# Scores gathered into one stretch per batch, with most of feed-forward-1 cut into 64-row quads, in an attention and feed-forward kernel on one core

## The chip, the cores and the metric

The kernel runs on one core of a Trainium2 chip. The metric is device time in microseconds (us) of one execution, lower is better. Most runs of one kernel agree within about 0.3%. The time includes about 2 us outside the span of the profile: 427 us of time goes with a span of 425 us. All runs of the changed and the edited kernels are of the fast state (mean granted TensorE clock 0.99 to 1.0), and runs of one table line were timed on the same chip as the kernel before.

Names of engines in the profile: PE is TensorE's matmuls, PEld its weight loads, DVE VectorE, ACT ScalarE, POOL GpSimd, SP SyncE (here only a queue for DMA).

## The reference, cut to what matters

```python
# q: (8 batches, 16 heads, 384, 64); k, v: (8, 4, 384, 64); w_in: (1024, 2048); w_out: (2048, 1024)
k, v = np.repeat(k, 4, axis=1), np.repeat(v, 4, axis=1)
scores = np.matmul(q, k.transpose(0, 1, 3, 2)) / np.sqrt(64)
attn = softmax(scores)
x = np.matmul(attn, v)                        # "AV"; then rows of all heads side by side: (3072, 1024)
h = np.maximum(x @ w_in, 0.0)                 # "feed-forward-1"
out = (h * h) @ w_out                         # "feed-forward-2"
```

The contraction of scores has 64 elements, that of everything else 128 or a multiple of it. So scores fill only half of the rows of the 128 x 128 array. The kernel lays one head's keys on rows 0 to 63 and another's on rows 64 to 127 and lets two matmuls of 64 rows run side by side, as two tiles of the array.

## The kernel before

A recorder collects every operation with what it reads and writes, orders TensorE's work by a model of time, and inserts semaphores. Per batch TensorE does 12 units of scores, 8 of AV (18 matmuls each), 16 tiles of feed-forward-1 (8 matmuls of 384 columns each) and 6 groups of feed-forward-2 (16 matmuls of 512 columns each). From batch 1 on, scores came in bursts of two units. A burst fills six of the eight banks of PSUM, and one wide exp empties them:

```python
    def burst_two(b, u):
        def sc(pe):
            for k0, cols in ((0, ((0, 512), (512, 768))), (1, ((0, 256), (256, 768)))):
                for c0, c1 in cols:
                    for x in range(2):            # x = 0: rows 0..63 of the array, x = 1: rows 64..127
                        flat = ps[:, 3 * x:3 * x + 3, :].rearrange("p n c -> p (n c)")
                        m = pe.matmul(flat[:, k0 * HC + c0:k0 * HC + c1],
                                      kT[b % 2][64 * x:64 * x + 64, u + k0, :],
                                      q_cols(b, (u + k0) // NJ, x, c0, c1))
            return m
        # ... PE writes banks 0..5; one ACT exp of 3072 elements a partition reads them all
```

Feed-forward-1 used the whole array, in banks 6 and 7, and split its work after the matmul between two engines:

```python
            def mm(pe):                            # one half of a tile: k0..k1 of 8 chunks
                for kc in range(k0, k1):
                    m = pe.matmul(bank(i)[:, 0:S], w_in_sb[:, kc, c * 128:(c + 1) * 128],
                                  xT[b % NXT][:, kc, :], start=(kc == 0), stop=(kc == NKC - 1))
                return m
                # ... after the last chunk:
                R.add("vector", lambda e: e.tensor_scalar_max(hr[r][:, :], bank(i)[:, 0:S], 0.0), ...)
                R.add("scalar", lambda e: e.activation(h2T[b % 2][:, c, :], hr[r][:, :], AF.Square), ...)
```

A list scheduler picks the next piece for TensorE; scores of batch b+1, AV of batch b+1 and feed-forward of batch b are mixed as they become ready:

```python
        if sc_q:
            # ... b > 0:
                ok = ok and not held & set(LOW)
                t = max(R.when(reads=score_reads(b, u) + score_reads(b, u + 1)) + 3.0 * (b == 2),
                        R.when(writes=[("bank", i) for i in LOW]))
        # ...
        ready = [x for x in cand if x[0] <= now + 0.05]
        what = min(ready, key=lambda x: x[1]) if ready else min(cand)
```

The softmax here doesn't subtract the row's maximum and nothing guards it: scores larger than these inputs give would overflow.

## Time and profile before

| | |
|---|---|
| time, median of 4 runs | 427.08 us (426.95 to 427.46) |
| span of the profiled run | 425.1 us |
| TensorE busy | 99% of the span |
| VectorE, ScalarE busy | 37%, 46% |
| score bursts in batches 1 to 7 | 42 |

Lines of the profile's page follow. Some records of matmuls are missing (755 of line 496 below, where the program has 784); a step that spans a missing record was read as two. First comes the table of busy times: busy us, share of the span, instructions of each engine. Then the chain of work that ended last, then groups of instructions: line, engine, operation, output<-inputs, shapes, count | busy us, mean ns of one | idle time of the engine before them.

```profile
PE 419.2 (99%) x3435; PEld 231.1 (54%) x3464; DVE 157.7 (37%) x332; ACT 194.8 (46%) x194; POOL 55.3 (13%) x68
...
PE 96%; DMA 1%; issue 1%; ACT 1%; POOL 1%; DVE 0%; POOLq 0%
...
L440 PE MATMUL ps<-xT,w_in_sb 128*128 128x384 bf16 x1024 | 174.8, 326 | 0.0
L496 PE MATMUL ps<-w_out_sb,h2T 128*128 128x512 bf16 (+2 forms) x755 | 167.5, 375 | 1.9 <-issue 0.5
L368 ACT ACTIVATE expT<-ps 128x3072 bf16<-128x3072 f32 x42 | 114.5, 2727 | 64.4 <-PE ps L358 63.7
...
L383 PE MATMUL ps<-v_aug,expT 128*128 128x65 bf16 x1152 | 41.2, 193 | 0.0
...
L358 PE MATMUL ps<-qT,kT 64*128 64x512 bf16 (+1 forms) x336 | 34.6, 325 | 0.0
```

TensorE has next to no idle time, and 96% of the chain is TensorE: only less work on TensorE, or denser work, can help. The "mean ns" of a matmul is no cost, as matmuls overlap. The cost is the step from one start to the next.

The timeline of TensorE in the kernel before. Columns: start us, us until the last of the run ends, engine, line, what, count.

```profile
128.60 0.82 PE L358 MATMUL ps<-qT,kT 64*128 64x512 bf16 x8
129.36 3.42 PE L440 MATMUL ps<-xT,w_in_sb 128*128 128x384 bf16 x20
132.62 1.26 PE L383 MATMUL ps<-v_aug,expT 128*128 128x65 bf16 x36
133.72 1.46 PE L440 MATMUL ps<-xT,w_in_sb 128*128 128x384 bf16 x8
135.11 0.82 PE L358 MATMUL ps<-qT,kT 64*128 64x512 bf16 x8
135.87 3.42 PE L440 MATMUL ps<-xT,w_in_sb 128*128 128x384 bf16 x20
```

Read it by start times. Twenty matmuls of line 440 start at 129.36 and the next kind at 132.62: 163 ns each. The Trainium skill ("TensorE: Matmul & The Clock Gate", Back-to-back issue gap) gives columns / 2.4 GHz + 2.5 ns for a single matmul with a warm clock, here 162.5 ns; the trace agrees. But the eight from 133.72 to 135.11, where a score burst follows, take 1.39 us instead of 1.30. The score burst from 135.11 to 135.87 takes 0.76 us, where its columns need 0.65. From the start times of single matmuls, the step into a burst is 258 ns after a 384-column matmul (163 elsewhere) and 312 after one of 512 columns (216 elsewhere); out of a burst it is 308 instead of 216. I call each such change between whole array and 64-row tiles a border. Over the 84 borders the median loss is 96 ns. The first step behind a border is about 10 ns slow as well (226 ns for a pair of 512 columns).

### The profile page before, as it was taken

Reading aid. Unit: us, or ns where it says so; the run is one execution under the profiler, and the core shown is the slowest. Engines: PE = TensorE matmul, PEld = TensorE weight load, DVE = VectorE, ACT = ScalarE, POOL = GpSimd, SP = SyncE. Lnnn points to the kernel's source line nnn. Section 1 sums busy time; section 2 is a strip of 40 time slices with the busy share of each in tenths; the row PEclk is TensorE's granted clock in tenths of the full one; section 3 lists DMA queues with packets and bytes.
Section 4 is the critical chain, followed back from the end, with each engine's and each line's share of the span. In section 5 each row is a group of like instructions: output and inputs, shape, how many; then the busy total and the mean of one; then the engine's idle time right before and its main releaser. Section 6 shows DMA issues by size and latency. Waiting matters only on the chain.

```text
span 425.1 us, 7813 instructions
## 1 busy us (share of the span) xinstructions
PE 419.2 (99%) x3435; PEld 231.1 (54%) x3464; DVE 157.7 (37%) x332; ACT 194.8 (46%) x194; POOL 55.3 (13%) x68
## 2 busy tenths in 40 slices
PE   8999999999999999999999999999999999999997
PEld 6665554555545555455554455544554465446544
DVE  3564331443324443244442344432441244114312
ACT  6957720477255773557745377552340034003300
POOL 8680001234012004004000000000000000000000
DMA  9999999999689179838918321033001100110012
GB/s 180 190 189 201 186 200 228 173 152 172 136 182 167 26 106 131 144 100 133 116 45 180 104 23 25 18 93 91 25 2 49 74 26 2 49 74 26 1 68 81
DMA packets 96915, 44.30 MB, mean 104 GB/s; under 512 B 77296, under 2 KB 90864, under 8 KB 96880
## 3 DMA queue, kind: packets, MB, share of 16 engines
q0 software_dynamic: 36544, 17.44, 32.2%
q1 hardware_dynamic: 59664, 25.86, 28.7%
q8 instruction: 27, 0.44, 0.4%
q10 hardware_dynamic: 672, 0.49, 0.4%
q14 instruction: 8, 0.07, 0.1%
HBM read 35.65 MB, written 12.58 MB: 113 GB/s over the span
## 4 chain that ended last, share of the span: by engine, by line
PE 96%; DMA 1%; issue 1%; ACT 1%; POOL 1%; DVE 0%; POOLq 0%
PE ps L440 40%; PE ps L496 39%; PE ps L383 8%; PE ps L358 7%; DMA q_st<-in_q_dram 1%; PE ps L337 1%; ACT expT L347 1%; PE ps L311 0%; PE ps L416 0%; PE ps L294 0%; POOL q_st L239 0%; POOL v_st L232 0%; DVE qT L318 0%; DVE y_sb L505 0%; POOL ident L523 0%
## 5 line engine op out<-in xcount | busy, mean ns | idle before, releaser
L440 PE MATMUL ps<-xT,w_in_sb 128*128 128x384 bf16 x1024 | 174.8, 326 | 0.0
L496 PE MATMUL ps<-w_out_sb,h2T 128*128 128x512 bf16 (+2 forms) x755 | 167.5, 375 | 1.9 <-issue 0.5
L368 ACT ACTIVATE expT<-ps 128x3072 bf16<-128x3072 f32 x42 | 114.5, 2727 | 64.4 <-PE ps L358 63.7
L440 PEld LDWEIGHTS ps<-xT,w_in_sb 128*128 128x128 bf16 x1024 | 97.1, 98 | 69.5 <-issue 6.8
L450 ACT ACTIVATE h2T<-hr 128x384 bf16<-128x384 f32 x128 | 64.5, 520 | 140.7 <-DVE hr L448 140.5
L496 PEld LDWEIGHTS ps<-w_out_sb,h2T 128*128 128x128 bf16 x784 | 73.7, 98 | 87.1 <-issue 5.1
L448 DVE TENSOR_SCALAR hr<-ps 128x384 f32<-128x384 f32 x128 | 71.2, 557 | 106.3 <-PE ps L440 106.3
L505 DVE COPY y_sb<-ps 128x512 f32<-128x512 f32 (+2 forms) x49 | 33.3, 681 | 122.6 <-PE ps L496 122.6
L383 PEld LDWEIGHTS ps<-v_aug,expT 128*128 128x128 bf16 x1152 | 39.3, 98 | 6.9 <-issue 0.6
L383 PE MATMUL ps<-v_aug,expT 128*128 128x65 bf16 x1152 | 41.2, 193 | 0.0
L398 DVE TENSOR_TENSOR o_sb<-ps,rinv 128x384 bf16<-128x384 f32 x64 | 35.6, 557 | 2.2
L358 PE MATMUL ps<-qT,kT 64*128 64x512 bf16 (+1 forms) x336 | 34.6, 325 | 0.0
L358 PEld LDWEIGHTS ps<-qT,kT 64*128 64x128 bf16 x336 | 13.0, 94 | 20.7 <-issue 6.3
L392 DVE RECIPROCAL rinv<-ps 128x6 f32<-128x6 f32 x64 | 12.2, 190 | 27.0 <-PE ps L383 27.0
L271 POOL COPY v_aug<-v_st 128x768 bf16<-128x768 bf16 x8 | 6.6, 831 | 84.1 <-PE ps L383 69.3
L347 ACT ACTIVATE expT<-ps 128x1024 bf16<-128x1024 f32 (+1 forms) x20 | 16.9, 981 | 0.7 <-PE ps L337 0.6
L266 POOL COPY k_dup<-k_st 128x1536 bf16<-128x1536 bf16 x7 | 10.3, 1470 | 42.7 <-DMA k_st<-in_k_dram 42.7
L239 POOL DMA_DIRECT2D q_st<-in_q_dram x17 | 14.8, 886 | 0.9 <-POOLq L751 0.8
L207 POOL DMA_DIRECT2D k_st<-in_k_dram x7 | 5.3, 758 | 39.1 <-DMA qT<-q_st 39.1
L337 PE MATMUL ps<-qT,kT 64*128 64x384 bf16 (+2 forms) x48 | 7.2, 330 | 0.6 <-DVE qT L318 0.2
L249 POOL DMA_DIRECT2D w_in_sb<-in_moe_w_in_dram x8 | 7.1, 895 | 0.0
L232 POOL DMA_DIRECT2D v_st<-in_v_dram x8 | 6.3, 790 | 0.1
(26 smaller groups left out, 41.5 us busy)
## 6 DMA issues: line engine op xcount, KB each, us to landing
out_dram<-y_sb SPq DMA_DIRECT2D x47, 256.0 KB, 2.0
q_st<-in_q_dram POOLq DMA_DIRECT2D x14, 384.0 KB, 8.5
w_in_sb<-in_moe_w_in_dram POOLq DMA_DIRECT2D x8, 512.0 KB, 14.3
w_out_sb<-in_moe_w_out_dram POOLq DMA_DIRECT2D x4, 1024.0 KB, 30.2
v_st<-in_v_dram POOLq DMA_DIRECT2D x8, 192.0 KB, 10.4
k_st<-in_k_dram POOLq DMA_DIRECT2D x7, 192.0 KB, 4.4
q_st<-in_q_dram POOLq DMA_DIRECT2D x3, 192.0 KB, 5.0
xT<-o_sb SPq DMA_TRANSPOSE x28, 2.9
```

The lines of the kernel that those rows point to most:

```text
L239: R.add("gpsimd", lambda g: g.dma_start(q_st[st][:, h0:h1, :], q[b, h0:h1].rearrange("h (p j) d -> p h (j d)", j=NJ)), writes=[("q_st", st ...
L347: R.add("scalar", lambda e: e.activation(dst, src, AF.Exp, scale=0.125), reads=keys, writes=[("expT", (b * NU + u) % NEX, t) for u, _, _ i ...
L358: m = pe.matmul(flat[:, k0 * HC + c0:k0 * HC + c1], kT[b % 2][64 * x:64 * x + 64, u + k0, :], q_cols(b, (u + k0) // NJ, x, c0, c1))
L368: R.add("scalar", lambda e: e.activation(dst, src, AF.Exp, scale=0.125), reads=keys, writes=[("expT", (n + m) % NEX, t) for m in range(2) ...
L383: m = pe.matmul(po[:, f - 6 * s2, 0:D + 1], w, v_aug[b % 2][:, g * NJ + j, 0:D + 1], start=(j == 0), stop=(j == NJ - 1))
L392: R.add("vector", lambda e: e.reciprocal(rinv[r].ap().unsqueeze(2), po[:, :, D:D + 1]), reads=[("bank", i)], writes=[("rinv", r)], cost=0.13)
L398: R.add("vector", lambda e: e.tensor_tensor(dst, srcv, rbv, ALU.mult), reads=[("bank", i), ("rinv", r)], writes=[("o_sb", o, s2)], cost=0.48)
L440: m = pe.matmul(bank(i)[:, 0:S], w_in_sb[:, kc, c * 128:(c + 1) * 128], xT[b % NXT][:, kc, :], start=(kc == 0), stop=(kc == NKC - 1))
L448: R.add("vector", lambda e: e.tensor_scalar_max(hr[r][:, :], bank(i)[:, 0:S], 0.0), reads=[("bank", i)], writes=[("hr", r)], cost=0.48)
L450: R.add("scalar", lambda e: e.activation(h2T[b % 2][:, c, :], hr[r][:, :], AF.Square), reads=[("hr", r)], writes=[("h2T", b % 2, c)], cost ...
L496: m = pe.matmul(bank(i)[:, 0:n], h2T[b % 2][:, c, i3 * 128:(i3 + 1) * 128], w_out_sb[:, c, c0:c1], start=(c == 0), stop=(c == NFC - 1))
L505: R.add("vector", lambda e: e.tensor_copy(ysl, bank(i)[:, 0:n]), reads=[("bank", i)], writes=[("y", yb)], cost=0.08 + n / 960)
```

## The change

Its intent is to have TensorE change between whole-array matmuls and 64-row tiles twice per batch instead of twelve times. To have something to run beside the scores in the same mode, feed-forward-1 is cut into 64-row halves. A "quad" works on four tiles in banks 4 to 7. In phases 0 and 1 the two halves of the array work on different tiles, in phases 2 and 3 they swap, so that each tile gets both halves of its contraction. Scores go in small pieces through banks 0 to 3. The run of scores and quads of one batch is called its stretch. AV and feed-forward-2 then run on the whole array. VectorE now makes the squares of the quads. The core of the diff:

```diff
-    NST, NEX, NXT, NHR, NY = 2, 8, 3, 4, 3
+    NST, NEX, NXT, NHR, NY, NO = 2, NU, 2, 4, 3, 6
...
-    def burst_two(b, u):      # (removed; scores use burst_small, two banks and exps of 1024 elements)
...
+    def quad(b, tiles):
+        rs, ends = [], {}
+        def part(phase, k0):
+            xs = ((0, 1), (2, 3), (1, 0), (3, 2))[phase]
+            def piece():
+                def mm(pe):
+                    for kc in range(k0, k0 + 4):
+                        for x in range(2):
+                            c, r = tiles[xs[x]], slice(64 * x, 64 * x + 64)
+                            m = pe.matmul(bank(4 + xs[x])[:, 0:S], w_in_sb[r, kc, c * 128:(c + 1) * 128],
+                                          xT[b % NXT][r, kc, :], start=(phase < 2 and kc == 0),
+                                          stop=(phase > 1 and kc == NKC - 1))
+                    return m
+                ...
+                for i in sorted(xs):          # after phases 2 and 3
+                    R.add("vector", ... e.tensor_scalar_max(hr[r][:, :], bank(4 + i)[:, 0:S], 0.0) ...)
+                for c, r in rs if phase == 3 else ():
+                    R.add("vector", ... e.tensor_tensor(h2T[:, c, :], hr[r][:, :], hr[r][:, :], ALU.mult) ...)
...
+            if b and not split:     # a stretch opens only at an edge, with four tiles or more left
+                ok = ok and at_edge and (u > 0 or pairs >= 8 * b and ff["b"] == b - 1 and len(ff["tiles"]) >= 4)
...
+                t = max(R.when(reads=reads) + 3.0 * (b == 2 and not split), R.when(writes=[...two banks...]))
...
+        if split:
+            inside = [x for x in cand if x[2] in ("sc", "ffn")]
+            if not at_edge or inside and min(inside)[0] <= now + 0.3:
+                cand = inside
```

In the resulting order 100 of the 128 feed-forward-1 tiles run as quads: 12 beside the scores of batch 1, 8 beside those of batch 2, 16 beside those of batches 3 to 7.

## The prediction

> **What bounds it now.** TensorE. The first table of the page gives PE 99% of the 425.1 us span; the chain of waits is 96% PE, with feed-forward-1 40%, feed-forward-2 39%, AV 8%, the score bursts of batches 1 to 7 7%. VectorE is busy 37%, ScalarE 46%. Start-to-start steps of matmuls in the trace: feed-forward-1 163 ns (384 columns), feed-forward-2 216 ns (512), AV 29 ns, a pair of 64-row score matmuls 109 ns per 256 columns. Each is columns/2.4 GHz plus about 2.5 ns, so there is no slack inside a run of one kind.
>
> **What the change removes.** The visible loss is at the border between whole-array matmuls and 64-row tiles. Into a burst the step is 258 ns where 163 is normal, or 312 where 216 is normal: 95 ns. Out of it 308 ns, where a 512 pair takes 216: 92 ns. The first pair inside takes 227 instead of 216. The Trainium skill ("TensorEngine Tiling (Array Packing)", Key Properties) says a change of tiling mode drains the array; this trace agrees, at about 94 ns. Before: 42 bursts, 84 borders, about 8.3 us with the slow first pairs. In the changed order of instructions I count 20 borders in batches 1 to 7 (two per batch, eight in batch 2, whose scores outlast its quads). 64 fewer: 64 x 94 ns = 6.0 us, and 0.4 us of slow first pairs. All of it is on the critical path, as PE never rests.
>
> **What it adds or moves.** 100 of 128 feed-forward-1 tiles run as quads: 1600 half-height matmuls in 800 pairs. The bursts show pairs at the rate of one whole-array matmul and weight loads (94 ns, two at once) hidden, so I expect 162 to 165 ns a pair: 0 to 1.5 us. Exps become 1024 elements wide, 1.06 us (batch 0) against half of 2.73: 18 x 1.06 = 19 us per stretch, under the stretch's 20.8 + 3.9 = 25 us of PE, so ScalarE should not stall PE. Squares move to VectorE: per quad four relus and four multiplies at a step of about 0.48 us (557 ns recorded, overlapping) = 3.9 us against 5.2 to 6.3 us of PE. It fits, but tightly at one place: two banks come free about 1.46 us after the last matmul start of a phase (0.36 release + 0.48 + 0.56 + signal), and the phase after next wants them after 1.46 us. Where no score piece lies between, up to 0.1 us waits: 0 to 2 us. AV begins behind a VectorE backlog of about 3 us; six banks and four feed-forward-2 matmuls cover most of it: about 0.5 us. Start and last batch stay as they were. w_in chunk 3 lands at 30.4 us and is wanted at about 30.6.
>
> **Prediction.** 427.1 - 6.4 + about 1.6 = **422.0 us**; 8 in 10: 419.8 to 425.6. Faster by over 2%: 0.04; within 2%: 0.90; slower by over 2%: 0.06.
>
> **What would show it.** Right: about 20 steps of 258 to 312 ns at borders; a quad pair's step at 162 to 165 ns; PE still 99%; VectorE's share up by about 10 points, ScalarE's down about 7; waits of PE's weight loads for VectorE and ScalarE summing under 3 us. Wrong: a pair step well over 165 ns; PE waits for the relus or the exps of several us; VectorE near full in the stretches.
>
> **What could make it wrong.** The multiply on two fp32 operands costing more than 0.5 us a step; half-height weight loads not hidden beside longer streams (each 10 ns on a pair costs 8 us); q/k transposes arriving late now that a batch wants all scores at once; the two-bank release being later than I read.

## The result, and the profile after

| kernel | time, median (range) | against the kernel before |
|---|---|---|
| before | 427.08 us (426.95 to 427.46) | |
| changed | 423.50 us (423.38 to 425.05) | 0.9923, 95% interval 0.9899 to 0.9947 |

A ratio here and below is the mean time of one kernel's fast runs over that of the other's of the same rounds, so it is not quite the ratio of the medians quoted. The change makes the kernel 0.8% faster: 3.6 us. That lies in the predicted range, and the verdict is "same" at the 2% line.

The profile fell on the slowest of the four runs (425.05 us). Its TensorE waited 1.6 us for the first queries at about 9 us, where its repeat (e5 below, 423.74 us) waited 0.6 us. From 11.05 us on its trace also records half the clock for 3.41 us, and e5's trace does not. In the thirteen traces such a stretch at half clock, before the work ends, follows only pauses of TensorE of 1.6 to 2.0 us (here, in e6, and twice in e3); no pause of 1.45 us or less has one. Four cases don't make a rule. Such differences of the start come and go in all kernels here. So I also compare the profiles from a fixed point on: from the run of feed-forward-1 ahead of batch 1's scores to the end of the last matmul. That is 397.4 us in the kernel before and 393.4 us in the changed one, 4.0 us less. The lines of its page:

```profile
PE 414.9 (98%) x4241; PEld 236.9 (56%) x4264; DVE 198.4 (47%) x432; ACT 155.3 (37%) x178; POOL 55.3 (13%) x68
...
PE 95%; DVE 2%; DMA 1%; issue 1%; POOL 1%; POOLq 0%
...
L347 ACT ACTIVATE expT<-ps 128x1024 bf16<-128x1024 f32 (+1 forms) x146 | 138.4, 1015 | 162.3 <-PE ps L337 162.0
L515 PE MATMUL ps<-w_out_sb,h2T 128*128 128x512 bf16 (+2 forms) x761 | 165.6, 374 | 1.2
L458 PE MATMUL ps<-xT,w_in_sb 64*128 64x384 bf16 x1600 | 148.1, 322 | 0.0
...
L337 PE MATMUL ps<-qT,kT 64*128 64x256 bf16 (+2 forms) x384 | 54.4, 328 | 1.1 <-ACT expT L347 0.9
L474 DVE TENSOR_TENSOR h2T<-hr 128x384 bf16<-128x384 f32 x100 | 48.8, 549 | 0.0
```

The timeline of TensorE in the stretch of batch 4, changed kernel, columns as before:

```profile
179.07 0.61 PE L337 MATMUL ps<-qT,kT 64*128 64x512 bf16 x4
179.51 1.46 PE L458 MATMUL ps<-xT,w_in_sb 64*128 64x384 bf16 x16
180.81 0.38 PE L337 MATMUL ps<-qT,kT 64*128 64x256 bf16 x4
181.03 1.46 PE L458 MATMUL ps<-xT,w_in_sb 64*128 64x384 bf16 x16
182.33 0.38 PE L337 MATMUL ps<-qT,kT 64*128 64x512 bf16 x2
```

Sixteen half-height matmuls from 179.51 to 180.81 are eight pairs in 1.30 us: 162.5 ns a pair, the rate of a whole-array matmul. Four score matmuls of 256 columns from 180.81 to 181.03 take 0.22 us. Nothing is lost where scores and quads meet. The step from a quad to a score or back is the plain 162, 109 or 216 ns of the matmul's own columns in all of the 217 places. So the loss of 96 ns before was the change of tiling and not the wait or the change of operands at the start of a group.

The same timeline at the end of batch 1's stretch, with the lines of VectorE and weight loads. "[... <-X]" is idle time before, and what ended it:

```profile
50.45 4.93 PE L363 MATMUL ps<-v_aug,expT 128*128 128x65 bf16 x143
51.28 1.95 DVE L474 TENSOR_TENSOR h2T<-hr 128x384 bf16<-128x384 f32 x4
53.15 0.19 DVE L372 RECIPROCAL rinv<-ps 128x6 f32<-128x6 f32 x1
...
53.98 1.27 PEld L363 LDWEIGHTS ps<-v_aug,expT 128*128 128x128 bf16 x35 [0.20 <-DVE o_sb L378]
...
55.88 0.10 PEld L363 LDWEIGHTS ps<-v_aug,expT 128*128 128x128 bf16 x1 [0.63 <-issue]
55.88 0.20 PE L363 MATMUL ps<-v_aug,expT 128*128 128x65 bf16 x1 [0.51 <-issue]
```

AV runs through its six free banks while VectorE still makes the last quad's squares (51.28 to 53.2). The seventh unit of AV needs a bank back and waits until 53.98, the eighth a little more: together 0.38 us. The last matmul of AV waits another 0.67 us, for "issue", that is for nothing that the profile shows.

In batch 2, TensorE and one line of VectorE:

```profile
100.25 1.27 PE L363 MATMUL ps<-v_aug,expT 128*128 128x65 bf16 x36
...
101.08 1.95 DVE L474 TENSOR_TENSOR h2T<-hr 128x384 bf16<-128x384 f32 x4
...
101.45 0.60 PE L337 MATMUL ps<-qT,kT 64*128 64x512 bf16 x4
...
102.96 0.39 PE L337 MATMUL ps<-qT,kT 64*128 64x256 bf16 x4 [0.91 <-ACT expT L347]
...
103.78 0.72 PE L363 MATMUL ps<-v_aug,expT 128*128 128x65 bf16 x18 [0.43 <-DVE o_sb L378]
...
104.56 0.81 PE L515 MATMUL ps<-w_out_sb,h2T 128*128 128x512 bf16 x3
...
105.30 0.61 PE L337 MATMUL ps<-qT,kT 64*128 64x512 bf16 x4
```

Here the stretch has run out of quads before its scores were done. From then on, scores (L337), AV (L363) and feed-forward-2 (L515) alternate, with a border each time, and TensorE waits 0.91 us for an exp and 0.43 us for an output of VectorE. With the excess read from single start times the waits of this place are 1.07, 0.50 and 0.08 us: 1.65 us. Only the first of the three is for an exp. Before the second, VectorE still made the squares of the last quad (101.08 to 103.03 us) and came late to AV's outputs, as in batch 1.

Adding up the steps beyond their plain length, after the start, the two profiles differ by: 64 borders fewer, 6.1 us; 64 first steps behind a border no longer 10 ns slow, 0.6 us; against that the waits just named, 1.05 us in batch 1 and 1.65 us in batch 2. That leaves 4.0 us of gain, against 4.0 us between the two profiles from the fixed point on and 3.6 us between the medians.

### The profile page after: what moved, and what is told of

Same layout as the page of the kernel before. It is cut to its first block, busy times and chain, and to the rows that moved or that the text cites. A ratio compares the mean times of both kernels' runs of the same rounds, so it can differ in the third digit from the quotient of the medians.

```text
span 423.1 us, 9473 instructions
## 1 busy us (share of the span) xinstructions
PE 414.9 (98%) x4241; PEld 236.9 (56%) x4264; DVE 198.4 (47%) x432; ACT 155.3 (37%) x178; POOL 55.3 (13%) x68
## 4 chain that ended last, share of the span: by engine, by line
PE 95%; DVE 2%; DMA 1%; issue 1%; POOL 1%; POOLq 0%
PE ps L515 39%; PE ps L458 31%; PE ps L421 9%; PE ps L363 8%; PE ps L337 8%; DMA q_st<-in_q_dram 1%; DVE h2T L474 1%; DVE hr L471 0%; PE ps L396 0%; PE ps L311 0%; DVE o_sb L378 0%; PE ps L294 0%; POOL q_st L239 0%; POOL v_st L232 0%; DVE qT L318 0%
## 5 line engine op out<-in xcount | busy, mean ns | idle before, releaser
L347 ACT ACTIVATE expT<-ps 128x1024 bf16<-128x1024 f32 (+1 forms) x146 | 138.4, 1015 | 162.3 <-PE ps L337 162.0
L515 PE MATMUL ps<-w_out_sb,h2T 128*128 128x512 bf16 (+2 forms) x761 | 165.6, 374 | 1.2
L458 PE MATMUL ps<-xT,w_in_sb 64*128 64x384 bf16 x1600 | 148.1, 322 | 0.0
L515 PEld LDWEIGHTS ps<-w_out_sb,h2T 128*128 128x128 bf16 x784 | 75.1, 98 | 86.6
L458 PEld LDWEIGHTS ps<-xT,w_in_sb 64*128 64x128 bf16 x1600 | 77.8, 94 | 52.4
L471 DVE TENSOR_SCALAR hr<-ps 128x384 f32<-128x384 f32 x100 | 51.1, 552 | 74.2 <-PE ps L458 74.2
L337 PE MATMUL ps<-qT,kT 64*128 64x256 bf16 (+2 forms) x384 | 54.4, 328 | 1.1 <-ACT expT L347 0.9
L474 DVE TENSOR_TENSOR h2T<-hr 128x384 bf16<-128x384 f32 x100 | 48.8, 549 | 0.0
L431 ACT ACTIVATE h2T<-hr 128x384 bf16<-128x384 f32 x28 | 14.6, 522 | 80.7 <-DVE hr L429 80.7
L363 PEld LDWEIGHTS ps<-v_aug,expT 128*128 128x128 bf16 x1152 | 37.7, 98 | 8.3 <-issue 3.5
L363 PE MATMUL ps<-v_aug,expT 128*128 128x65 bf16 x1152 | 40.6, 194 | 1.0 <-issue 0.5
L421 PE MATMUL ps<-xT,w_in_sb 128*128 128x384 bf16 x224 | 37.9, 326 | 0.0
L421 PEld LDWEIGHTS ps<-xT,w_in_sb 128*128 128x128 bf16 x224 | 21.7, 98 | 14.1 <-issue 0.2
L337 PEld LDWEIGHTS ps<-qT,kT 64*128 64x128 bf16 x384 | 17.4, 94 | 16.8 <-issue 3.4
L429 DVE TENSOR_SCALAR hr<-ps 128x384 f32<-128x384 f32 x28 | 15.5, 556 | 18.6 <-PE ps L421 18.6
## 6 DMA issues: line engine op xcount, KB each, us to landing
v_st<-in_v_dram POOLq DMA_DIRECT2D x8, 192.0 KB, 10.5
```

The costliest lines, as they stand in the source:

```text
L337: mm = pe.matmul(ps[:, base + x, m * wide:(m + 1) * wide], kT[b % 2][64 * x:64 * x + 64, u, :], q_cols(b, u // NJ, x, c0, c0 + wide))
L347: R.add("scalar", lambda e: e.activation(dst, src, AF.Exp, scale=0.125), reads=keys, writes=[("expT", (b * NU + u) % NEX, t) for u, _, _ i ...
L363: m = pe.matmul(po[:, f - 6 * s2, 0:D + 1], w, v_aug[b % 2][:, g * NJ + j, 0:D + 1], start=(j == 0), stop=(j == NJ - 1))
L458: m = pe.matmul(bank(4 + xs[x])[:, 0:S], w_in_sb[r, kc, c * 128:(c + 1) * 128], xT[b % NXT][r, kc, :], start=(phase < 2 and kc == 0), stop ...
L471: R.add("vector", lambda e, r=r, i=i: e.tensor_scalar_max(hr[r][:, :], bank(4 + i)[:, 0:S], 0.0), reads=[("bank", 4 + i)], writes=[("hr", ...
L474: hr_read[r] = (R.add("vector", lambda e, c=c, r=r: e.tensor_tensor(h2T[:, c, :], hr[r][:, :], hr[r][:, :], ALU.mult), reads=[("hr", r)], ...
```

## The experiments

All outputs are right. Medians, with the median of the kernel before in the same session. The last column is the profiled run from the fixed point on, which leaves the differences of the start out (before: 397.4; changed, first profile: 393.4):

| run | edit | time us (range) | before | ratio (95%) | fixed point on, us |
|---|---|---|---|---|---|
| e1_whole | quads as whole-array matmuls | 445.2 (444.8 to 447.0) | 427.48 | 1.0424 (1.040 to 1.0447) | 414.9 |
| e2_before_dve | kernel before, squares on VectorE | 427.75 (427.2 to 428.2) | 427.48 | 1.0001 (0.9988 to 1.0014) | 397.5 |
| e3_act_sq | changed, squares on ScalarE | 425.97 (424.4 to 427.5) | 427.48 | 0.9958 (0.9939 to 0.9978) | 395.7 |
| e4_fixAB | changed, both repairs | 421.24 (420.7 to 421.7) | 427.48 | 0.9849 (0.9833 to 0.9864) | 390.7 |
| e5_after | the changed kernel again | 423.95 (423.5 to 424.2) | 427.47 | 0.9917 (0.9905 to 0.9929) | 393.9 |
| e6_fixA | first repair alone | 423.22 (422.7 to 424.5) | 427.47 | 0.9906 (0.9892 to 0.9919) | 392.6 |
| e7_fixB | second repair alone | 422.74 (421.8 to 423.0) | 427.47 | 0.9886 (0.9873 to 0.9899) | 391.8 |
| e8_tail_quads | last batch as quads too | 424.79 (424.0 to 425.7) | 427.47 | 0.9938 (0.9924 to 0.9951) | 395.0 |
| e9_shift | 27 matmuls more at the start | 423.4 (422.8 to 424.2) | 427.09 | 0.9909 (0.9894 to 0.9925) | 394.3 |
| e10_fixAB_again | as e4 | 420.94 (420.5 to 421.1) | 427.09 | 0.9849 (0.9836 to 0.9863) | 390.7 |
| e11_inter | second repair, AV mixed with feed-forward-2 | 420.44 (420.2 to 421.2) | 427.09 | 0.9843 (0.983 to 0.9857) | 390.7 |

The theory was: the gain is the borders taken away, at 96 ns each, and what is missing of it was lost to waits in batches 1 and 2. Rivals were that the gain comes from the other parts of the change (narrower exps, squares on VectorE, the new order), and that the missing part is a small loss spread over all quads.

### e1_whole: put the borders back

```diff
-                    for kc in range(k0, k0 + 4):
-                        for x in range(2):
-                            c, r = tiles[xs[x]], slice(64 * x, 64 * x + 64)
-                            m = pe.matmul(bank(4 + xs[x])[:, 0:S], w_in_sb[r, kc, ...], xT[b % NXT][r, kc, :], ...)
+                    t = (0, 2, 1, 3)[phase]
+                    for kc in range(k0, k0 + 4):
+                        m = pe.matmul(bank(4 + t)[:, 0:S], w_in_sb[:, kc, tiles[t] * 128:(tiles[t] + 1) * 128],
+                                      xT[b % NXT][:, kc, :], start=(kc == 0), stop=(kc == NKC - 1))
```

> The changed kernel with the quads of the stretches as whole-array matmuls (four of 128 rows instead of eight of 64), order otherwise the same. The instruction order then has 232 borders between whole array and 64-row tiles in batches 1 to 7 instead of 20. Theory (each border costs about 96 ns, nothing else matters): 212 x 96 ns = 20.4 us slower than the changed kernel, about 443.9 us, with a step of about 258 ns wherever a quad's matmul is followed by a score, and no change elsewhere. Rival (the gain comes from the long stretches, the narrower exps or the squares on VectorE, and the borders are incidental): within 2 us of the changed kernel's 423.5 us.

It took 445.2 us, 21 us more than the changed kernel (423.95 in e5, another session with the same median before). The timeline of TensorE in the stretch of batch 4 of e1_whole:

```profile
190.04 0.39 PE L337 MATMUL ps<-qT,kT 64*128 64x512 bf16 x2
190.37 1.47 PE L457 MATMUL ps<-xT,w_in_sb 128*128 128x384 bf16 x8
191.77 0.39 PE L337 MATMUL ps<-qT,kT 64*128 64x256 bf16 x4
192.10 0.82 PE L457 MATMUL ps<-xT,w_in_sb 128*128 128x384 bf16 x4
```

Eight whole-array matmuls and the border behind them take 1.40 us (190.37 to 191.77), where eight pairs took 1.30. Four score matmuls of 256 columns take 0.33 us, where they took 0.22. The 232 borders have a median excess of 96 ns. Summed, they cost 23.4 us, 20.9 us more than the 20 borders of e5's profile. The two profiles differ by 21.0 us from the fixed point on. What else differs cancels: 10 ns at more first steps is some 1.4 us more, and 1.3 us of e5's waits, 1.1 us of it in batch 1's AV, is gone. The borders account for nearly all of the difference, so the price of 96 ns is shown both by taking borders away and by adding them. The same run shows that one stretch per batch without the quads would have been a loss of 4.2%.

### e2_before_dve: only move the squares

```diff
-                R.add("scalar", lambda e: e.activation(h2T[b % 2][:, c, :], hr[r][:, :], AF.Square), ...)
+                R.add("vector", lambda e: e.tensor_tensor(h2T[b % 2][:, c, :], hr[r][:, :], hr[r][:, :], ALU.mult), ...)
```

> The kernel before with its squares moved from ScalarE to VectorE, nothing else. Theory: PE has no wait for ScalarE or VectorE there, so it is the same within 0.5 us (426.6 to 427.6 us), with ScalarE's share down to about 31% and VectorE's up to about 52%. Rival (moving the squares is part of the gain): faster by 1 us or more.

The time is the same, 1.0001, and so is the profile from the fixed point on (397.5 against 397.4 us). The busy line of its page:

```profile
PE 419.5 (98%) x3437; PEld 231.3 (54%) x3464; DVE 228.9 (54%) x460; ACT 134.1 (31%) x66; POOL 55.5 (13%) x68
```

Some 60 to 70 us of work moved from ScalarE to VectorE changes nothing where TensorE is the limit. This rival falls.

### e3_act_sq: move the squares back in the changed kernel

```diff
                 for c, r in rs if phase == 3 else ():
-                    hr_read[r] = (R.add("vector", lambda e, c=c, r=r: e.tensor_tensor(h2T[:, c, :], hr[r][:, :], hr[r][:, :], ALU.mult), ...),)
+                    R.add("scalar", lambda e, c=c, r=r: e.activation(h2T[:, c, :], hr[r][:, :], AF.Square), ...)
```

> The changed kernel with the quads' squares on ScalarE again. Theory: ScalarE then has 18 x 0.94 + 16 x 0.45 = 24 us of work in a stretch of 25 us of PE, so scores begin to wait for exps, above all in batches 1 and 2 whose stretches hold 12 and 8 tiles; VectorE's backlog at the start of AV goes, and with it the 0.4 us wait of AV in batch 1. Net 0.5 to 4 us slower than the changed kernel. Rival (VectorE's backlog is what ate the gain): 1 us or more faster than the changed kernel.

It is about 2 us slower than the changed kernel (0.9958 against 0.9917 of the kernel before, in two sessions; 395.7 us from the fixed point on against 393.4 and 393.9). AV's wait for VectorE in batch 1 is gone, as expected. But the scheduler, told that ScalarE makes the squares, also chose another order. The scores of batch 1 now outlast their quads, with six more borders, and its AV is mixed with scores and feed-forward-2; batch 2 has two more borders. So this run does not move the squares alone, and it does not show which of the two took that wait away (e11 below loses it by the order alone). The long waits are all in batch 2; the timeline of TensorE and ScalarE there in e3_act_sq:

```profile
102.41 0.61 PE L337 MATMUL ps<-qT,kT 64*128 64x256 bf16 x6
...
103.30 0.52 ACT L431 ACTIVATE h2T<-hr 128x384 bf16<-128x384 f32 x1 [1.17 <-DVE hr L429]
103.73 3.75 ACT L347 ACTIVATE expT<-ps 128x1024 bf16<-128x1024 f32 x4
...
104.79 0.39 PE L337 MATMUL ps<-qT,kT 64*128 64x512 bf16 x2 [1.77 <-ACT expT L347]
```

Where scores have to run without quads, they follow one another at the pace of ScalarE. Here ScalarE also has squares, which themselves wait for VectorE. In the stretches of batches 3 to 7 there is no long step even so: my estimate of 24 us of ScalarE's work in 25 us of TensorE's was tight, but it held. So the squares on ScalarE cost something only in the first two batches, whose stretches are short.

One thing in this trace is easily overlooked: it records half the clock from 106.32 to 109.73 us, right behind these waits: a matmul of 512 columns goes at 427 ns there instead of 216, one of AV at 55 instead of 29. By the plain lengths of the steps in it, this costs about 1.6 us, most of what the profile lost. Four of the other runs have a mean clock of 0.996, and where they lost it no trace shows. The only run at a clock of 1.0 took 424.41 us, 0.5 us above e5's median. So most of the 2 us is likely a matter of the clock, and only the rest one of waits and borders. That the waits set it off is likely too, but not shown.

### e4_fixAB, e6_fixA, e7_fixB: repair batches 1 and 2

Repair A puts four matmuls of feed-forward-2 before the seventh AV of batches 1 and 2; later batches already have that order. Repair B opens the stretch of batch 2 when 12 tiles are left instead of 8. It may wait for its transposed queries, and its scores then end inside the stretch.

```diff
+        if what[2] == "av" and av_q[0][0] and av_q[0][1] == 6 and len(ff["down"]) == 24 and not ff["tiles"]:
+            what = (now, 5, "ffn")                                                      # A
...
+        if not split and sc_q and sc_q[0] == (2, 0) and ff["b"] == 1 and len(ff["tiles"]) == 12 and not ff["now"]:
+            f_head = None                                                               # B
-                t = max(R.when(reads=reads) + 3.0 * (b == 2 and not split), ...)
+                t = max(R.when(reads=reads), ...)                                       # B
```

> The changed kernel with two repairs of its order: the stretch of batch 2 starts when 12 tiles of feed-forward-1 are left instead of 8, so its scores end inside it (14 borders in place of 20), and in batches 1 and 2 four matmuls of feed-forward-2 stand before the seventh AV, as in later batches. Theory (the gain that was expected and did not come was lost in batches 1 and 2: 1.65 us of waits for exps and 0.6 us of borders in batch 2, 0.4 to 1.0 us in batch 1's AV): 2 to 3 us faster than the changed kernel, 420.5 to 421.5 us, less up to 0.6 us if the transposed queries of batch 2 come after the earlier start. Rival (the missing part is spread over all stretches): no more than 0.5 us faster.

> The changed kernel again, as the yardstick of the repairs on the same chip. All theories: 423.0 to 424.0 us; its profile should again show the waits in the AV of batch 1 and in batch 2 that the first profile showed (about 0.4 us for VectorE and 1.65 us for exps and outputs), and may or may not show again the 0.67 us before the last AV matmul of batch 1, for which that profile names no releaser.

> The first repair alone: in batches 1 and 2 four feed-forward-2 matmuls stand before the seventh AV. Theory (AV waits there for banks that VectorE frees late): 0.4 us faster than the changed kernel, 1.0 us if the unnamed 0.67 us goes too; the waits of AV's weight loads for VectorE in batch 1 gone. Rival (an order effect without that cause): no change.

> The second repair alone: the stretch of batch 2 starts with 12 feed-forward-1 tiles left. Theory: waits for exps in batch 2 gone (1.65 us) and 6 borders fewer (0.6 us), 0.4 us given back for VectorE's backlog at AV of batch 2: 1.4 to 2.3 us faster than the changed kernel. Rival (the transposed queries of batch 2 are what holds its stretch up): PE waits for them at the start of the stretch by about as much as it saves, under 0.7 us faster.

Both repairs give 421.24 us, and 420.94 us in a second session (e10). Against 423.95 us for the changed kernel in e5 that is 2.7 to 3.0 us, the expected size; from the fixed point on it is 2.7 to 3.2 us. Alone they give 0.7 us (A) and 1.2 us (B) by the medians, 0.8 to 1.3 and 1.6 to 2.1 us from the fixed point on. A's interval overlaps that of e5 (0.9892 to 0.9919 against 0.9905 to 0.9929), so A alone is supported by its trace and not settled by its time. e7 itself still shows the waits of batch 1 (0.22, 0.13 and 0.70 us), a new one of 0.25 us at the seventh AV of batch 2, and one of 0.44 us near the start of batch 2's stretch. In that last one the third piece of scores waits for an exp: in ScalarE's order of work the square of the last whole-array tile (80.70 us in e4) stands before the first exp (81.13 us). The first half of the transposed queries had landed 0.7 us before the stretch began (79.25 against 79.99 us in e4; the second half landed at 83.87 us, and no score waits for it), so the rival named for e7 falls. The timeline of TensorE at the end of batch 2's stretch, both repairs (e10):

```profile
99.12 0.38 PE L337 MATMUL ps<-qT,kT 64*128 64x256 bf16 x4
99.44 3.45 PE L363 MATMUL ps<-v_aug,expT 128*128 128x65 bf16 x108
102.73 1.03 PE L515 MATMUL ps<-w_out_sb,h2T 128*128 128x512 bf16 x4
103.59 1.26 PE L363 MATMUL ps<-v_aug,expT 128*128 128x65 bf16 x36
```

The last scores end and AV follows at once; compare the alternation above. AV's first 108 matmuls take 3.29 us, the four of feed-forward-2 0.86 us, and nothing waits. What e10 still has is the 0.44 us wait for an exp and 0.31 us unnamed in batch 1's AV. e5's profile of the changed kernel had, as its expectation said, 1.07, 0.50 and 0.08 us in batch 2, and 0.24, 0.13 and 1.00 us in batch 1. It also had 0.23 us in the first quad, which e9 explains.

### e8_tail_quads: quads with nothing beside them

```diff
-        n = 4 if split else 1
+        n = 4 if split or ff["b"] == B - 1 else 1        # in two places
```

> The changed kernel with feed-forward-1 of the last batch, 16 tiles, as quads too, though no score stands beside them: 512 pairs... of half-height matmuls at their densest, banks released without score pieces between, and no AV between the last quad and feed-forward-2. Theory: pairs at 162 to 163 ns as whole-array matmuls, so nothing for the quads themselves; two more borders, 0.2 us; up to 0.1 us a phase where two banks are released late (0 to 1 us in 16 phases); and about 0.4 us because feed-forward-2 wants the last squares before VectorE has made them. Together 0.4 to 1.5 us slower than the changed kernel. Rival (quads themselves are slower than whole-array matmuls and scores hide it): 2 us or more slower, with pair steps over 170 ns.

(The text says 512 pairs; the 16 tiles make 128.) It is 0.8 us slower than e5 (1.1 us from the fixed point on). Of the 128 pairs none has a long step, and pairs go at 162.5 ns here too, so neither the half-height matmuls nor the release of two banks costs anything, even at its tightest. The added time stands at one place, the change to feed-forward-2, in its timeline:

```profile
399.31 1.02 DVE L471 TENSOR_SCALAR hr<-ps 128x384 f32<-128x384 f32 x2 [0.28 <-PE ps L458]
399.92 3.13 PEld L515 LDWEIGHTS ps<-w_out_sb,h2T 128*128 128x128 bf16 x16 [1.04 <-DVE hr L471]
400.15 3.18 PE L515 MATMUL ps<-w_out_sb,h2T 128*128 128x512 bf16 x14 [0.88 <-DVE hr L471]
```

Feed-forward-2 waits 0.9 us for its bank, because two relus in a row (399.31 to 400.3) come after the last phase. I had expected it to wait for the squares, and that did not occur. In the changed kernel AV stands between, in other banks, and covers this wait in every batch.

### e9_shift: what the unnamed wait is

In the profiles of the changed kernel, e5, e7 and e8, the last matmul of batch 1's AV waits 0.67 to 1.00 us with no releaser named, always before AV matmul 143 of 144. In e6 and e4, with four matmuls of feed-forward-2 put in before it, it stands five AV matmuls earlier, before number 138, and is 0.32 us. In the four profiles checked for it (after, e5, e8, e6) it ends 2.3 to 2.5 us after the start of a 16 KB packet on the DMA queue that the profile names "instruction". The changed kernel has 33 packets there, the one before 27, while TensorE has 800 more matmuls and 800 more weight loads: in both it is one packet for 256 to 258 of TensorE's recorded matmuls and weight loads. The theory was that TensorE has run out of fetched instructions.

```diff
-    warm_up(27, 2.77)
+    warm_up(54, 2.77, 64)      # 54 matmuls of 64 columns in place of 27 of 128
```

> The changed kernel with its first warm-up of 27 matmuls of 128 columns made of 54 matmuls of 64 columns: the same time, but 27 matmuls and 27 weight loads more ahead of everything. It asks what the unnamed wait in batch 1's AV is, which stood before AV matmul number 143 (counted from 0) in four profiles and came 2.4 us after a 16 KB packet of the instruction queue had begun. Theory (TensorE has run out of fetched instructions, as AV eats them at one per 15 ns): the wait moves to 27 matmuls earlier, before AV matmul 116, and again ends 2.4 us after the packet; the total stays within 1 us of the changed kernel, as the wait may grow, shrink or meet another one. Rival (something of the AV itself, its last exps or banks): the wait stays before AV matmul 143.

Neither side was right about the place. The wait is gone from AV, at 423.4 us. The packet now starts at 50.95 us, 0.7 us after AV's start, where it started 3.3 us after it in e5. That is more than the 54 added instructions explain by the pace of AV. The edit left AV's data and banks as they were, so the wait depends on where AV stands in the stream of instructions and not on them (e9 has one profile, but the wait also moved in e4, e6 and e10). That it is the fetching is the likely reading (the constant 2.4 us speaks for it), but the rule that sets the place is open.

This profile has another long wait, in the first quad of batch 0's tiles:

```profile
32.40 0.83 PE L458 MATMUL ps<-xT,w_in_sb 64*128 64x384 bf16 x8 [1.45 <-DMA w_in_sb<-in_moe_w_in_dram]
...
33.05 0.40 PE L337 MATMUL ps<-qT,kT 64*128 64x256 bf16 x4
```

The second phase of that quad wants w_in chunk 3, which landed at 32.27 us in this run. As an excess over the plain step it is 1.61 us. In e5 the same excess was 0.23 us, in e8 0.58 us, in e11 0.21 us, in the first profile none. The kernel before shows none. A quad asks for two chunks where a tile asks for one, so the change moved this demand forward; what the wait costs varies from run to run with the loads at the start.

### e11_inter: AV not in one block

```diff
+        if what[2] == "av" and av_q[0][0] and av_q[0][1] > 1 and last == "av2" and ff["down"] and not ff["tiles"] and not ff["now"]:
+            what = (now, 5, "ffn")
+        last = what[2]
```

with repair B as above.

> The kernel of e4 again, as the yardstick of e11 on the same chip: 421.2 us within 0.5.

> The batch 2 repair as in e4, and in every batch from the third AV on, four feed-forward-2 matmuls between two AVs instead of AV in one block. Theory (VectorE's backlog at the start of AV and the fetching of instructions both cost only because AV runs through 144 matmuls in 4.3 us): no wait of AV's weight loads for VectorE and no unnamed wait in any AV, 0.3 us faster than e10, that is 420.6 to 421.2 us. Rival: mixing AV with feed-forward-2 costs something at each of the 7 x 13 changes of kind; then 0.3 us or more slower than e10.

The timeline of TensorE at the start of batch 1's AV in e11_inter:

```profile
48.85 1.27 PE L363 MATMUL ps<-v_aug,expT 128*128 128x65 bf16 x36
49.95 1.02 PE L515 MATMUL ps<-w_out_sb,h2T 128*128 128x512 bf16 x4
50.82 0.71 PE L363 MATMUL ps<-v_aug,expT 128*128 128x65 bf16 x18
```

Two units of AV take 1.10 us and one 0.55 us (50.82 to 51.37, the next start), as in a block, so changing between AV and feed-forward-2 costs nothing. No AV waits for VectorE, and the unnamed wait is gone although an instruction packet starts amid this AV (52.04 us). Five new waits of 0.08 us stand before the first feed-forward-2 matmuls of batches 3 to 7. The medians say 0.5 us over e10, but the ratios, 0.9843 and 0.9849, overlap, and from the fixed point on the two profiles are the same (390.65 and 390.73 us): what is saved in batch 1 is given back in small waits elsewhere, 0.2 us of them for w_in chunk 3. So the waits are gone as expected, and the gain is not. The best versions, e10 and e11, are 1.5 to 1.6% faster than the kernel before and about 0.7% faster than the changed one.

## Why the prediction was right or wrong, point by point

- **Range and class: right, in part by luck.** 423.5 us was measured, 422.0 us predicted, 419.8 to 425.6 us given. The prediction allowed about 1.6 us for losses. The waits came to 2.7 us, and the two largest heads of the allowance, pair rate and release of banks, came out as zero: 1.07 us lay in a place that was ruled out (the exps) and 0.67 us in none that was named.
- **The bound: right.** TensorE was 98 to 99% busy before and after; e2 shows that moving the other engines' work alone does nothing.
- **What is removed: right in count and size.** 84 borders before and 20 after, 96 ns each (94 predicted). The removed part measured 6.1 + 0.6 us against 6.0 + 0.4 predicted; the slow first steps on the whole-array side were not counted. e1 confirms it from the other side.
- **Pair rate: right.** 162.5 ns; the term "0 to 1.5 us" came out as zero.
- **Release of two banks: mis-sized, harmless.** "0 to 2 us" came out as zero, also in e8. The slow release exists, but it is seen only where feed-forward-2 follows a quad at once (0.9 us in e8).
- **AV behind VectorE's backlog: right in kind, too small.** 0.38 us in batch 1 and 0.50 us in batch 2, against "about 0.5 us" in all.
- **"ScalarE should not stall PE": this step failed for batch 2.** I compared 19 us of exps with the 25 us of a stretch with 16 tiles. I had counted from the instruction order that batch 2's scores outlast its quads, and charged the extra borders for it, but not the waits. With 8 tiles the stretch has about 8 x 1.3 + 3.9 = 14.3 us, less than the exps. The wait for an exp cost 1.07 us, the largest missing term. With the waits of AV for VectorE in the same place it is 1.65 us. e7 took these away, at the price of new waits of 0.44 and 0.25 us.
- **Missing altogether: the unnamed wait in batch 1's AV**, 0.67 to 1.00 us, and the earlier demand on w_in chunk 3. I had called the latter tight (landing 30.4 us, wanted 30.6 us) without a cost; it was 0 to 1.6 us by run.
- **Signs to look for.** VectorE's share rose by 10 points (37 to 47%) and ScalarE's fell by 9 (46 to 37%, "about 7" said). TensorE's weight loads waited 3.2 us for the two engines from 27.4 us on, a little over the 3 us that was to be the limit. This sign is a poor one: the kernel before has 10.5 us of such waits, and its matmuls lose nothing by them. A wait on matmuls and one with no name had to be looked for as well.

## What to carry to other kernels

In these traces a change between whole-array matmuls and row tiles costs the same 96 ns each way, whatever runs on either side. Count the changes, and cut large matmuls into row-tile pairs if that lets small ones run beside them: the cut itself cost nothing here. When work is gathered into a stretch, compare the engine that follows (here the exps) with the shortest stretch, not the typical one. And when a gain comes out smaller than its mechanism, add up the steps beyond their plain length by place: here most of the shortfall stood in two batches of eight, and two small edits of the order gave it back (the second is clear by its time, the first by its trace alone). Look at the granted clock by place too: in e3 3.41 us at half the clock look at first like the cost of moved work.

## What the Trainium skill lacked or had wrong

- "TensorEngine Tiling (Array Packing)", Key Properties, says that a change of tiling mode drains the array, but not what that costs. The runs show 96 ns at each border, into and out of 64-row tiles, after matmuls of 65, 384 and 512 columns alike, 10 ns more at the first step behind it, and none between different work in the same mode.
- "TensorE: Matmul & The Clock Gate", Back-to-back issue gap, gives about 131 ns per matmul of 512 columns as the sustained spacing of a stream of weight loads and matmuls, and says that columns / 2.4 GHz + 2.5 ns counts too much there. The trace shows 216 ns for 512 columns in such a stream, 163 ns for 384: the formula holds and the 131 ns does not.
- The same page, Part 3, has speedups for row tiles with small contractions. It lacks the use shown here: two 64-row halves of different tiles of a large contraction go at 162.5 ns a pair of 384 columns, the rate of one whole-array matmul, weight loads hidden.
- "Runtime: NRT & Kernel Launch", Instruction fetch mechanics, says that an engine's sequencer fetches its instructions ahead in blocks of 16 KiB, and that crossing from one block to the next is mostly hidden. The only stall of this kind that it names is at a taken branch; it has none in straight code such as this, and no cost. The runs show a wait of 0.3 to 1.0 us in a dense block of 144 matmuls of 65 columns with their weight loads, ending 2.4 us after a 16 KB instruction packet began; it is probable, not proved, that fetching is the cause.
